# The same steps in a new order: replacing the written-out schedule of a two-branch kernel (attention with memory, and a long convolution)

## The chip, the cores and the metric

The kernel runs on 1 core of one Trainium2 chip. The metric is device time in microseconds (us), the median of several executions. Lower is better. A core has PE (TensorE, the matrix unit, with PEld its weight loads), ACT (ScalarE), DVE (VectorE), POOL (GpSimd) and SP (SyncE, which here issues every transfer). Each takes its own instructions strictly in order and waits for the others through semaphores.

## What is computed

The input `A_x` has 2048 tokens of 512 channels. The output is a gated mix of two branches. Cut to what matters:

```python
g = sigmoid((x * gate_w).sum(-1, keepdims=True))
a = A(x)      # 32 heads of 16; four segments of 512 tokens
b = B(x)      # a long convolution over the 2048 tokens, per channel
return g * a + (1 - g) * b

# A, for segment s and each head:
p = softmax(q @ k.T * scale + causal_mask)
o = gh * (phi(q) @ M) / (phi(q) @ z) + (1 - gh) * (p @ v)
M, z = M + phi(k).T @ v, z + phi(k).sum(0)     # memory for the next segment
a = o @ wo
# B:
K[d, l] = real(sum over n of C[d,n] * exp(dt[d] * A[d,n] * l) * dt[d] * B[d,n])
b = causal_conv(x, K) + x * Dskip              # by Fourier transforms in the reference
```

## The kernel before, in words

**Attention.** `do_xT` (L710) brings x transposed into memory: segment 0 by a plain load and PE transposes (L728), segments 1 to 3 by one transposing transfer each, issued on SP at L713. `project` (L979) makes q and k for one of four head groups of 8 heads, `seg_tokens` (L918) makes v. `scores` (L1008) runs five tiles per head group and segment, 80 in all. Each is a set of score matmuls into four PSUM banks (the same four every time), one exponential on ACT over 128 x 2048 (L1069), a causal mask (added by PE before the exponential in the first eight head groups, multiplied in by DVE at L1081 in the last eight), and the products with v. `norm` inside it ends with the DVE multiplication at L1044. `seg_state` (L937) updates the memory and `ophase` (L1100) adds the memory's part and transposes the outcome for the last product.

**Convolution.** `ssm_prep` (L734) and `ssm_powers` (L785) compute complex exponentials and then square them repeatedly, ten times in two halves; every power gets a table tile, of which a part is copied by a transfer inside the on-chip memory (the "copies of the power tables"). `tables` (L1136) multiplies them out on DVE (L1164, L1167, L1171) and PE turns them into kernel values ("lag"). `x_level1` (L845) makes the first transform level of x and stores it to a scratch in memory. `tail` (L1221) then goes through 16 frequency groups for each of two halves of the channels ("a" and "b"). For each group SP loads three operands (two parts of a constant named c_DNM, and the scratch), PE makes X and K, both are evicted, the halves of X are swapped by two 64 KB transfers, DVE multiplies (L1273), PE makes the inverse step V, and that is evicted and moved to its rows by a transfer.

**End.** Sixteen output blocks, eight per half, each add the attention's last product (`fina`, `finb`: all heads and segments must be there) and the convolution's last transform (`fira`, `firb`) in one PSUM bank. The two evictions of a block multiply by the gate (L229 on ACT, L230 on DVE) and every second block stores 256 KB.

**What sets the order.** All matmuls are recorded through one helper line (L687), and all plain transfers through L222. `evac` (L224) records a PSUM eviction that can run either on ACT (L226, or L229 with a scale) or on DVE (L227, or L230). The graph holds 1798 steps, numbered in the order in which the program records them. A string `ORDER` (L366 to L456) lists all 1798 numbers: `build_kernel` (L1362) reads it and `replay` (L235) goes through it. The text after a number gives slots, that is which buffer of a pool or which PSUM bank a new tile gets, and the letter a or v puts an eviction on ACT or DVE:

```python
order.append((int(w[0].rstrip("av")), "ACT" if w[0][-1] == "a" else "DVE", [int(v) for v in w[1:]]))
...
for T in o.tiles:
    if T.slot is None:
        T.pool.take(T, next(slots))
```

So each engine's queue is the list cut down to that engine's steps. A step waits for the steps whose outcome it reads, and for the former users of the slots it takes; `emit` (L264) writes the semaphores. SP waits as well: a transfer that is not ready holds all that stand behind it on SP.

## Time and profile before

| what | value |
|---|---|
| runs (median; lowest to highest) | 313.3 us; 310.99 to 313.7 |
| profiled execution: span | 311.0 us |
| lowest run beside it | 310.99 us |
| PE, DVE, ACT busy | 264.8, 260.2, 262.7 us |
| first score exponential begins, last one ends | 24.5, 274.5 us |
| transfers issued on SP | 283 |

How to read it: the slices of the page divide the span in 40 parts and give each engine's busy share in tenths. The windows give busy time and instruction counts of each engine in chosen stretches, the granted PE clock, and the DMA engines' share and rate. A group is one source line on one engine with its count, busy time, mean duration in ns, and the idle time just before its instructions with what ended it. Of a transfer, the timeline's row on SP is the time that SP was held by the issue, not the time until the data landed. The last exponential's end is the end of the row of L1069 that begins at 272.66 and takes 1.88 us.

### The profile page before, as it was taken

To read this page: it belongs to the slowest core of one execution; us is meant where nothing else is said; L and a number is where in the kernel's file an instruction comes from. 1 tells how busy PE (TensorE), PEld (TensorE's weight loads), DVE (VectorE), ACT (ScalarE), POOL (GpSimd) and SP (SyncE) were. 2 spreads that over 40 slices of the span, in tenths; PEclk is the share of its full clock that TensorE was granted. 3 is DMA by queue.
4 is the path that set the end of the run, shared out by engine and by line. 5 is a ranking of instruction groups with operands and counts; after the bars stand their busy time and mean duration, and the time that the engine had idled before them with its cause. 6 is when DMAs were issued, how large, how long until landed. Compare 5 with 4: busy or idle time off the path is not lost.

```text
span 311.0 us, 10366 instructions
## 1 busy us (share of the span) xinstructions
PE 264.8 (85%) x4397; PEld 185.1 (60%) x4430; DVE 260.2 (84%) x642; ACT 262.7 (84%) x320; POOL 3.1 (1%) x9
## 2 busy tenths in 40 slices
PE   2678788788779789998999898999999988799991
PEld 1433355454435547676766574676677666579991
DVE  1999899999998889998999868888999898862152
ACT  2999999999999979987999898999999999861150
POOL 2000000000000000000001000000000000000000
PEclk9995689999968779999999999999999999979997
DMA  6878522431232545465555657637555667511143
GB/s 145 280 176 160 142 87 70 124 118 52 83 110 77 160 121 155 147 197 157 158 173 192 199 159 229 196 95 228 156 197 186 200 200 217 168 52 48 38 137 102
DMA packets 54926, 45.82 MB, mean 147 GB/s; under 512 B 22624, under 2 KB 50272, under 8 KB 54880
## 3 DMA queue, kind: packets, MB, share of 16 engines
q1 hardware_dynamic: 54880, 45.16, 49.8%
q8 instruction: 35, 0.57, 0.8%
q14 instruction: 11, 0.09, 0.1%
HBM read 26.92 MB, written 6.29 MB: 107 GB/s over the span
## 4 chain that ended last, share of the span: by engine, by line
ACT 42%; PE 41%; issue 7%; DVE 4%; DMA 3%; SPq 1%; another core or an unknown queue 0%; DVEq 0%; ACTq 0%
PE psum L687 40%; ACT sb L1069 23%; ACT sb L226 13%; ACT sb L795 2%; DMA sb<-sb 1%; DVE sb L227 1%; DMA sb<-c_DNM 1%; DMA sb<-c_ident 1%; SPq L222 1%; ACT sb L803 1%; ACT sb L1000 1%; DVE sb L1273 1%; ACT sb L949 1%; DVE sb L1121 0%; ACT L888 0%
## 5 line engine op out<-in xcount | busy, mean ns | idle before, releaser
L687 PE MATMUL psum<-sb 128*128 128x17 bf16 (+12 forms) x4309 | 257.5, 225 | 32.5 <-ACT sb L1069 14.4
L687 PEld LDWEIGHTS psum<-sb 128*128 128x128 bf16 (+3 forms) x4342 | 178.2, 97 | 109.7 <-issue 29.7
L1069 ACT ACTIVATE sb<-psum 128x2048 bf16<-128x2048 f32 x80 | 151.9, 1899 | 6.7 <-PE psum L687 6.4
L226 ACT ACTIVATE sb<-psum 128x512 bf16<-128x512 f32 (+2 forms) x155 | 88.1, 625 | 8.6 <-PE psum L687 8.1
L227 DVE CAST sb<-psum 128x512 bf16<-128x512 f32 (+1 forms) x47 | 31.3, 676 | 4.8 <-PE psum L687 4.8
L1164 DVE TENSOR_TENSOR sb<-sb 128x512 bf16<-128x512 bf16 (+3 forms) x52 | 33.5, 654 | 0.0
L1167 DVE TENSOR_TENSOR sb<-sb 128x512 bf16<-128x512 bf16 (+3 forms) x52 | 33.3, 650 | 0.0
L1171 DVE TENSOR_TENSOR sb<-sb 128x512 bf16<-128x512 bf16 (+3 forms) x52 | 33.3, 656 | 0.0
L1081 DVE TENSOR_TENSOR sb<-sb 128x1024 bf16<-128x1024 bf16 (+1 forms) x40 | 22.5, 575 | 3.4 <-ACT sb L1069 3.3
L1273 DVE TENSOR_TENSOR sb<-sb 128x1024 bf16<-128x1024 bf16 x32 | 21.6, 678 | 2.6 <-DMA sb<-sb 1.9
L230 DVE TENSOR_SCALAR sb<-psum,sb 128x256 bf16<-128x256 f32 x18 | 8.4, 482 | 16.4 <-PE psum L687 15.2
L229 ACT ACTIVATE sb<-psum,sb 128x256 bf16<-128x256 f32 x14 | 6.2, 472 | 16.8 <-PE psum L687 8.8
L1044 DVE TENSOR_TENSOR sb<-psum,sb 128x256 bf16<-128x256 f32 x32 | 13.3, 418 | 0.3
L795 ACT ACTIVATE sb<-sb 128x512 f32<-128x512 f32 x18 | 11.6, 658 | 0.0
L1041 DVE RECIPROCAL sb<-psum 128x16 f32<-128x16 f32 x32 | 8.0, 251 | 2.3 <-PE psum L687 2.0
L1121 DVE TENSOR_TENSOR sb<-psum,sb 128x512 bf16<-128x512 f32 x12 | 8.2, 686 | 0.2
L743 PE MATMUL psum<-sb 128*128 128x128 bf16 x24 | 3.0, 310 | 6.0 <-DMA sb<-c_ident 5.4
L796 DVE TENSOR_TENSOR sb<-sb 128x256 f32<-128x256 f32 x18 | 7.5, 418 | 0.6 <-ACT sb L795 0.5
L949 ACT ACTIVATE sb<-psum 128x512 bf16<-128x512 bf16 x12 | 7.5, 622 | 0.3 <-PE psum L946 0.3
L1000 ACT ACTIVATE sb<-sb 128x512 bf16<-128x512 bf16 x12 | 7.5, 629 | 0.0
L227 DVE COPY sb<-psum 128x1024 bf16<-128x1024 bf16 x3 | 2.1, 686 | 6.4 <-PE psum L743 6.4
L797 DVE SCALAR_TENSOR_TENSOR sb<-sb 128x256 f32<-128x256 f32 x18 | 7.4, 415 | 0.0
(66 smaller groups left out, 102.0 us busy)
## 6 DMA issues: line engine op xcount, KB each, us to landing
sb<-c_DNM SPq DMA_DIRECT2D x32, 320.0 KB, 3.5
sb<-c_DNM SPq DMA_DIRECT2D x32, 192.0 KB, 3.0
sb<-sb SPq DMA_DIRECT2D x84, 64.0 KB, 2.6
scr_Z<-sb SPq DMA_DIRECT2D x16, 256.0 KB, 2.3
sb<-scr_Z SPq DMA_DIRECT2D x32, 128.0 KB, 3.1
sb<-sb SPq DMA_DIRECT2D x32, 128.0 KB
sb<-in_A_x_dram SPq DMA_DIRECT2D x5, 512.0 KB, 4.6
out_dram<-sb SPq DMA_DIRECT2D x8, 256.0 KB, 2.2
```

Of the source, the lines that this page charges most:

```text
L226: fa = lambda e: e.activation(dst(), src(), ACT.Copy)
L227: fd = lambda e: e.tensor_copy(dst(), src())
L687: mm = lambda e, o_, l, r_, st, sp, **kw: e.matmul(o_, lhsT=l, rhs=r_, start=st, stop=sp, skip_group_check=True, **kw)
L795: op("ACT", ("As", 512), lambda e, sq=sq, Z=Z: e.activation(ap(sq, n=512), ap(Z, n=512), ACT.Square), r=[Z], w=[sq], key=PW[h] + PWS * k)
L949: op("ACT", ("Ax", 512), lambda e: e.activation(ap(ek, n=512), ap(P, n=512), ACT.Exp), r=[P], w=[ek])
L1044: op("DVE", ("V1", 256), lambda e: e.tensor_tensor(ap(o1, gi * 16, [[128, 4], [32, 4], [1, 16]]), ap(T, dims=[[68, 4], [17, 4], [1, 16]]), ...
L1069: o = op("ACT", ("Ax", 2048), lambda e, P=P, pT=pT: e.activation(ap(pT, n=2048), ap(P, n=2048), ACT.Exp, scale=0.25), r=[P], w=[pT])
L1081: op("DVE", ("V2", 128 * nb), lambda e, pT=pT, dims=dims: e.tensor_tensor(ap(pT, dims=dims + [[1, 128]]), ap(pT, dims=dims + [[1, 128]]), ...
L1164: op("DVE", ("V2" if n > 1 else "V1", 256 * n), lambda e: e.tensor_tensor(run(tile, ne, dst, 1), run(tile, ne, src, sstep), ap(pw, cl * 51 ...
L1167: op("DVE", ("V2" if n > 1 else "V1", 256 * n), lambda e: e.tensor_tensor(run(t2, n, 0, 1), run(tile, ne, src, sstep), ap(pw, cl * 512 + 2 ...
L1171: op("DVE", ("V2" if n > 1 else "V1", 256 * n), lambda e: e.tensor_tensor(D_(), D_(), ap(t2, n * 128, [[-n * 128, 2], [2 * n, 64], [1, 2 * ...
L1273: op("DVE", ("V2", 1024), lambda e, Y=Y, XAB=XAB, K3=K3: e.tensor_tensor(ap(Y, dims=[[512, 2], [1, 512]]), ap(XAB, dims=[[512, 2], [1, 512 ...
```

## The change

Only the string `ORDER` is replaced. The same 1798 numbers stand in another order, with other slots, and other letters for the evictions. The change's own words: "Same steps, memory and transfers; order of all steps, engines of evictions and slots written anew, with the time that SP takes to begin each transfer counted in". Nothing of a step itself changes.

```diff
 ORDER = """
-9/0 10/1 391/1 15/0 29/0 0/0 23/0/0 24v 30/1 193/0 13/4 14/2 21/0 12/3 11/5 27/1/1 25/2/2 189/0 54/0 31/8 32/0 33/6
-38/2 39/3 57/3 34 190 35 7/0 37/11 20/0 1226/1 28a 36 17/0 45/8 40/4 41 55/4 44/5 26v 46/7 42 173/7 43 48/0 50/9 18/0
...
+9/0 10/1 0/0 23/0/0 24v 15/0 29/0 31/0 32/1 38/2 39/3 37/4 30/5 40/6 33/7 41 14/2 13/3 34 42 35 27/1/1 43 12/4 28a
+11/5 36 21/0 189/0 190 54/0 25/2/2 26a 173/0 7/0 49/8 53/0 176/0 45/9 50/10 44/11 48/1 46/12 47 51/13 52 57/3 177/0
...
```

What the two strings make of the queues, counted from them:

| what | before | after |
|---|---|---|
| instructions of PE steps, ACT, DVE, SP | 551, 317, 642, 283 | 551, 303, 656, 283 |
| output evictions on ACT (L229) / DVE (L230) | 14 / 18 | 0 / 32 |
| evictions of X, K and V of the tail on ACT, of 96 | 61 | 59 |
| q and k evictions on ACT | 30 of 32 | 26 of 32 |
| ACT instructions ahead of the first score exponential | 30 | 36 |
| ACT instructions up to and with the last one | 298 | 298 |
| identity load, place on SP | 4th | 3rd |
| loads of wq, wk, wv, places on SP | 18th, 14th, 15th | 13th, 14th, 16th |
| the three transposes, places on SP | 19th, 26th, 32nd | 15th, 20th, 28th |
| segment that each of them brings | 1, 2, 3 | 1, 3, 2 |
| first copy of a power table on SP | 22nd | 21st |
| first step of `tables` on DVE (a copy into a table) | 60th | 65th |

## The prediction

> **What bounds the kernel now.** I read the page first: busy shares, slices, costliest groups.

> ```profile
> span 311.0 us, 10366 instructions
> PE 264.8 (85%) x4397; PEld 185.1 (60%) x4430; DVE 260.2 (84%) x642; ACT 262.7 (84%) x320; POOL 3.1 (1%) x9
> DVE  1999899999998889998999868888999898862152
> ACT  2999999999999979987999898999999999861150
> L687 PE MATMUL psum<-sb 128*128 128x17 bf16 (+12 forms) x4309 | 257.5, 225 | 32.5 <-ACT sb L1069 14.4
> L1069 ACT ACTIVATE sb<-psum 128x2048 bf16<-128x2048 f32 x80 | 151.9, 1899 | 6.7 <-PE psum L687 6.4
> L226 ACT ACTIVATE sb<-psum 128x512 bf16<-128x512 f32 (+2 forms) x155 | 88.1, 625 | 8.6 <-PE psum L687 8.1
> L227 DVE CAST sb<-psum 128x512 bf16<-128x512 f32 (+1 forms) x47 | 31.3, 676 | 4.8 <-PE psum L687 4.8
> L1273 DVE TENSOR_TENSOR sb<-sb 128x1024 bf16<-128x1024 bf16 x32 | 21.6, 678 | 2.6 <-DMA sb<-sb 1.9
> L230 DVE TENSOR_SCALAR sb<-psum,sb 128x256 bf16<-128x256 f32 x18 | 8.4, 482 | 16.4 <-PE psum L687 15.2
> L229 ACT ACTIVATE sb<-psum,sb 128x256 bf16<-128x256 f32 x14 | 6.2, 472 | 16.8 <-PE psum L687 8.8
> ```

> Three engines have the same 260 us of work in 311 us, and ACT and DVE are full nearly everywhere but at both ends. ACT's row is a chain of 80 score exponentials (L1069, 1.90 us each) with evictions between them, so I use these "exps" as milestones, and read busy time in windows that begin where the 1st, 25th, 29th, 33rd, 37th, 45th, 53rd and 80th begin.

> ```profile
> core 0: us, PE busy (x) PEld busy (x) DVE busy (x) ACT busy (x) POOL busy (x), PEclk, DMA share, GB/s
> 0.00:24.50 24.50, 13.66 (x109) 8.32 (x112) 17.66 (x55) 18.20 (x33) 1.88 (x7) 0.98 0.74 203
> 24.50:102.30 77.80, 63.83 (x1243) 36.60 (x1256) 74.55 (x192) 75.89 (x96) 0.00 (x0) 0.87 0.38 100
> 102.30:116.30 14.00, 10.74 (x174) 6.76 (x160) 11.56 (x38) 11.90 (x15) 0.00 (x0) 0.76 0.49 140
> 116.30:133.00 16.70, 16.32 (x233) 12.07 (x234) 16.21 (x31) 15.78 (x23) 0.00 (x0) 1.00 0.51 150
> 133.00:152.60 19.60, 17.96 (x476) 14.00 (x475) 18.56 (x56) 16.49 (x24) 0.00 (x0) 1.00 0.60 186
> 152.60:178.50 25.90, 23.54 (x471) 16.30 (x473) 24.86 (x45) 24.22 (x30) 1.22 (x2) 1.00 0.58 176
> 178.50:204.60 26.10, 23.84 (x393) 16.75 (x396) 20.67 (x52) 24.33 (x28) 0.00 (x0) 1.00 0.64 189
> 204.60:272.70 68.10, 63.24 (x981) 45.95 (x985) 62.03 (x150) 65.22 (x59) 0.00 (x0) 1.00 0.61 185
> 279.00:304.60 25.60, 25.45 (x260) 23.33 (x260) 8.80 (x19) 7.04 (x16) 0.00 (x0) 1.00 0.26 78
> ```

> Window length less ACT busy is ACT's idle time: 6.3 us before the first exp, 1.9 up to the 25th, then 2.1, 0.9, 3.1, 1.7 and 1.8 in the five windows to 204.6, and 2.9 to the last exp. So ACT sets the time of the last exp (272.7), with 14.4 us of idle on the way, 9.6 of it from 102.3 to 204.6, where the convolution's steps come in. From 279 PE alone works: the 16 output blocks, which need all attention heads. SP's transfers hardly show. The rows of DMA issues (size, median us from issue to landing), and of waits for them (us in total, times, longest), are:

> ```profile
> sb<-sb SPq DMA_DIRECT2D x84, 64.0 KB, 2.6
> sb<-c_DNM SPq DMA_DIRECT2D x32, 192.0 KB, 3.0
> DVE sb L1273 <- DMA sb<-sb: 1.9, 4, 1.3
> PEld psum L687 <- DMA sb<-c_DNM: 0.7, 1, 0.7
> ```

> **The change, part by part.** All 1798 steps stay; their order on every engine, the eviction engine and the slots change. I counted each engine's new queue, pricing every instruction at its own duration in the profiled execution (an overlap with its predecessor taken off), or, where it changed engine, at the mean of its shape there.

> *ACT's work.* 303 evictions and activations instead of 317; the 14 output evictions at L229 (6.2 us in all) go to DVE. Those lay behind the last exp, under PE's last 25 us, so they buy nothing. Up to and with the last exp both queues hold 298, 250.0 us before and 250.6 after (mainly 6 fewer evictions of 512, and 2 more of 1024, 2 more copies of 512 and 4 of 256): +0.6 us on the path.

> *DVE's work.* 642 to 656 instructions, 260.2 to 267.4 us; up to the last normalisation (L1044 of the last head group) 249.3 to 251.4. In the last part DVE takes all 32 output evictions: 32 x 0.48 = 15.4 us beside PE's 25.5, hidden. What would lay this open is an output block waiting for its PSUM bank; with two evictions (0.96 us) to 1.6 us of PE per block that does not occur.

> *The start.* These rows of the timeline (start, length, what) carry it.

> ```profile
> 2.33 0.43 SPq L222 DMA_DIRECT2D sb<-c_ident  x1
> 5.37 1.92 PE L743 MATMUL psum<-sb 128*128 128x128 bf16 x16 [5.37 <-DMA sb<-c_ident]
> 6.44 0.69 DVE L227 COPY sb<-psum 128x1024 bf16<-128x1024 bf16 x1 [6.44 <-PE psum L743]
> 6.96 0.23 ACT L865 ACTIVATE sb<-sb 128x32 f32<-128x32 bf16 x1 [1.16 <-DMA sb<-in_A_beta_dram]
> 7.96 0.95 ACT L763 ACTIVATE sb<-sb 128x256 f32<-128x256 f32 x2 [0.77 <-DVE sb L762]
> 8.82 1.01 ACT L226 ACTIVATE sb<-psum 128x1024 bf16<-128x1024 bf16 x1
> 10.15 1.28 ACT L772 ACT_TABLE_LOAD   x1
> 11.85 5.99 SPq L713 DMA_TRANSPOSE sb<-in_A_x_dram  x1
> 23.59 3.56 SPq L713 DMA_TRANSPOSE sb<-in_A_x_dram  x1
> 30.10 3.08 SPq L713 DMA_TRANSPOSE sb<-in_A_x_dram  x1
> ```

> The identity moves from fourth to third on SP, one issue or 0.54 us earlier, and the first PE, DVE and L763 steps with it (L763 to about 7.1, since L865 now stands behind it). ACT then does two evictions of 1024 (1.0 each) instead of one ahead of its table load, which falls at about 9.6 instead of 10.15. Idle on ACT up to the load: 10.15 - 2.9 of work - 1.28 for the first load = 6.0 before; 9.6 - 3.5 - 1.28 = 4.8 after. I take 0.9 us of these 1.2. ACT then has 36 instructions (18.5 us) instead of 30 (14.5) ahead of the first exp, so that starts at 24.5 + 4.0 - 0.9 = 27.6. That is work done earlier, no loss.

> *SP.* 283 transfers in both. The three transposes stood 19th, 26th and 32nd in SP's queue and stand 15th, 20th and 28th; they hold SP for 5.99, 3.56 and 3.08 us, while nothing behind them goes out. Moved past: the loads of wv, of the block mask and of the mask column by the first, three copies of the power tables and two stores to the scratch by the second. Followed by hand (about 0.54 us per plain issue, the first transpose held for 6 us as the first row shows behind full loads, the second for 3.6 to 6), the first two hold SP from 8.3 to about 14.5 and from 17.5 to 21 or 23, wv lands near 19 (wanted at 21), and the first copy near 24 to 27 (wanted by DVE at 29, behind 21.1 us of its work). The third cannot go out before a copy that waits for DVE's 60th instruction (28.6): issue 29.9, landing 36 by the third row. Its first reader, the gates of segment 2, stands 30th in PE's queue and waits for an eviction on ACT until 37.7 anyway. Queued behind it on PE are the projection and the scores that ACT's 53rd and 55th instruction need. Cover is 1.7 us; beyond it each us of delay is one on ACT. I take nothing for it; the ends are 0 and, if the third holds as long as the first (5.99 for 3.3), 2.7 - 1.7 = 1 us of loss.

> [...]

> *The middle.* For the same exps, work of ACT / DVE / PE in us, old to new (DVE and PE: what must be done before the exp can run; PE at 0.43 ns per column, near the 0.44 of the window 279 to 304.6, 25.45 us for 58,368 columns, and short ones at 27 ns):
> - exps 1 to 29: ACT 87.8 to 86.8, DVE 83.0 to 83.7, PE 62.1 to 63.4
> - 29 to 33: ACT 15.8 to 15.2, DVE 16.2 to 14.0, PE 15.8 to 14.9
> - 33 to 37: ACT 16.6 to 19.0, DVE 22.9 to 22.0, PE 16.6 to 19.5
> - 37 to 45: ACT 24.2 to 23.2, DVE 24.1 to 23.3, PE 22.6 to 21.5
> - 45 to 53: ACT 24.3 to 21.7, DVE 21.0 to 22.1, PE 22.7 to 21.7
> - 53 to 80: ACT 65.2 to 64.6, DVE 62.0 to 63.8, PE 59.4 to 60.2

> In the old order DVE's work ahead of the 37th to 45th exp exceeds ACT's by 3 us, and there ACT waits; in the new one DVE stays 0.5 us below at the first exp and 1.2 or more afterwards. In return 33 to 37 carries more of ACT and PE at once.

> *The sum*, each stretch its fullest engine plus the idle of that engine in the old window: first exp 27.6; to the 29th 86.8 + 4.0 = 90.8; 15.2 + 0.9 = 16.1; PE 19.5 + 1.6 = 21.1; DVE 23.3 + 1.0 = 24.3; 21.7 + 1.8 = 23.5; 64.6 + 2.9 = 67.5. The last exp starts at 270.9 instead of 272.7. From there 38.3 us were left; PE's work behind the last exp falls from 29.5 to 28.8 us, of which I count the 0.4 that stood among the output blocks (one inverse step, 1024 columns): 37.9. Span 308.8, or 2.2 less. The span, 311.0, is that of the fastest of the three runs; the median, 313.3, lies 2.3 above. So 313.3 - 2.2 = 311.1.

> **The rivals.**
> *The middle flows.* If DVE's lead is all that stopped ACT, idle from 102.3 to 204.6 falls to the share of the two long windows (1.9 + 2.9 of 145.9 us, 3.3%): 3.4 us instead of the 8.0 in my sum, 306.5. For it: from 24.5 to 102.3 ACT runs at 98% beside a DVE at 96%. Against it: PE is at 92 to 98% from 116 to 152, and the wait rows of L1069 and L226 name PE, not DVE.
> *Transfers come late.* Place: the operand loads of the convolution (c_DNM) and the half swaps (sb<-sb 64 KB) ahead of L1273. For each transfer I added the work of the waiting engine between the last instruction that the transfer must wait for and the one that uses it: under 4 us in 14 cases before, 22 after. Each us missing is a stall. If a transfer takes 4 us with its issue, what is missing sums to 10.8 us before and 15.7 after, 4.9 more; at 4.5 us 20.6 and 28.2, 7.6 more: 318.7. It makes the kernel slower by over 1% from about 4.1 us on. Against it: the rows say 2.6 and 3.0 us, and only 2.6 us of waits; for it: those are medians, and the new order gives SP's queue in tighter sequence.
> *Nothing moves.* ACT's work is the same to 0.6 us, SP's cost was hidden, and the gains at the start go in new waits: 313.3. [...]

> **How the numbers follow.** My forecast has 0.46, the free middle 0.24, late transfers 0.22, nothing 0.08. About 1% is what a measurement of this kernel can tell from no change: 310.2 to 316.4. The forecast's own range is 308 to 314, some 0.16 of its chance below 310.2. Faster: 0.24 + 0.16 = 0.40; within: 0.30 + 0.08 = 0.38; slower: 0.22. The range goes from 303 (the free middle, with the rest of the start's gain and some more) to 317.5, which leaves the worst late transfers out.

> **What would show it.** First exp at 27 to 28.5; ACT idle from the 29th to the 53rd exp under 7 us (7.5 before); the 33rd to 37th exp the one stretch that lengthens (20 to 22 us); the last exp at 270 to 272; PE's last block of work again 25 us, with all evictions at L230. Wrong: a wait on a DMA among the longest waits of PE or DVE; the gates of segment 2 later than 39; ACT idle above 16 us between the first and the last exp.

## The result, and the profile after

The changed kernel takes 329.6 us (median of 4 runs, 327.33 to 331.56); the kernel before, run beside it, 312.85 (310.99 to 313.7). The ratio is 1.0523 [1.0449, 1.0596]: 5.2% slower, 16.8 us, where 311.1 was forecast. A ratio leaves out executions over 1.5% above the fastest of their kernel, a median does not, so the two can differ. The profiled execution has a span of 329.6, 18.6 more than the one of before.

The page of the changed kernel, first the engines and the slices, then groups, then the queue that brings instructions:

```profile
span 329.6 us, 10405 instructions
PE 274.6 (83%) x4430; PEld 186.2 (56%) x4430; DVE 269.4 (82%) x656; ACT 258.1 (78%) x306; POOL 3.2 (1%) x9
ACT  3999979978999289896999949899998998680000
PEclk9999789979996759999999979999999999699998
L687 PE MATMUL psum<-sb 128*128 128x17 bf16 (+11 forms) x4342 | 268.1, 230 | 40.2 <-ACT sb L1069 15.0
L1069 ACT ACTIVATE sb<-psum 128x2048 bf16<-128x2048 f32 x80 | 151.2, 1890 | 11.3 <-PE psum L687 10.5
L226 ACT ACTIVATE sb<-psum 128x512 bf16<-128x512 f32 (+2 forms) x149 | 85.2, 622 | 12.1 <-PE psum L687 11.6
L227 DVE CAST sb<-psum 128x512 bf16<-128x512 f32 (+1 forms) x55 | 36.5, 673 | 9.7 <-PE psum L687 8.7
L230 DVE TENSOR_SCALAR sb<-psum,sb 128x256 bf16<-128x256 f32 x32 | 14.4, 480 | 9.7 <-PE psum L687 9.2
q8 instruction: 35, 0.57, 0.8%
```

The work is close to what the prediction counted: ACT 258.1 busy, DVE 269.4 (267.4 counted), all 32 output evictions on DVE. What grew is idle time. ACT's slices have a 2 and a 4 where before they were 7 or more, and PEclk, the granted clock, dips close to them. The windows, cut at the 1st, 25th, 29th, 33rd, 37th, 45th, 53rd and 80th exponential as in the prediction, show where:

```profile
core 0: us, PE busy (x) PEld busy (x) DVE busy (x) ACT busy (x) POOL busy (x), PEclk, DMA share, GB/s
0.00:28.60 28.60, 15.74 (x73) 7.53 (x74) 20.45 (x61) 22.29 (x39) 1.87 (x7) 1.00 0.78 200
28.60:116.90 88.30, 68.62 (x1314) 38.98 (x1313) 73.45 (x194) 75.56 (x96) 0.66 (x1) 0.87 0.34 87
116.90:129.40 12.50, 10.98 (x159) 7.41 (x157) 10.96 (x31) 11.71 (x13) 0.00 (x0) 0.68 0.41 116
129.40:145.70 16.30, 16.24 (x225) 12.21 (x222) 16.02 (x34) 15.27 (x21) 0.00 (x0) 1.00 0.48 145
145.70:168.40 22.70, 19.51 (x480) 14.18 (x479) 19.27 (x51) 18.83 (x30) 0.00 (x0) 1.00 0.59 173
168.40:197.00 28.60, 24.09 (x543) 16.52 (x542) 23.35 (x45) 23.57 (x28) 0.65 (x1) 0.94 0.50 152
197.00:221.10 24.10, 22.68 (x323) 15.42 (x321) 21.78 (x57) 22.00 (x23) 0.00 (x0) 1.00 0.68 197
221.10:292.40 71.30, 66.70 (x984) 47.20 (x983) 63.29 (x144) 64.73 (x56) 0.00 (x0) 0.95 0.59 177
298.50:324.10 25.60, 24.53 (x253) 22.50 (x251) 15.72 (x36) 0.00 (x0) 0.00 (x0) 1.00 0.29 87
```

ACT's work up to the last exponential is 254.0 us, 252.0 before. Its idle time from the first to the last one is 32.1 us (12.7, 0.8, 1.0, 3.9, 5.0, 2.1, 6.6), 14.4 before. So 17.7 us of idle and 2.0 of work put the last exponential at 292.4 instead of 272.7. The rest of the kernel is 1.1 us shorter (37.2 from there to the end, 38.3 before).

Whom did ACT and DVE wait for? The rows of the waits (us in total, times, longest), first before, then after:

```profile
ACT sb L226 <- PE psum L687: 9.8, 15, 1.7
DVE sb L227 <- PE psum L687: 6.8, 10, 1.9
PE psum L687 <- issue: 6.5, 13, 1.3
ACT sb L1069 <- PE psum L687: 6.4, 14, 1.5
```

```profile
ACT sb L226 <- PE psum L687: 21.1, 14, 6.3
DVE sb L227 <- PE psum L687: 19.3, 13, 7.5
PE psum L687 <- issue: 13.1, 5, 3.0
ACT sb L1069 <- PE psum L687: 10.5, 22, 2.3
```

On ACT's and DVE's evictions there are about as many waits as before (14 for 15, 13 for 10), but single ones of 6.3 and 7.5 us, and PE itself stood five times for 13.1 us with "issue" as releaser: nothing that the profile shows held it. They belong together. `tables` ends, for each of four groups of 128 channels, in eight PE steps ("lag" steps) of 32 weight loads and 32 matmuls of 20 columns each, 512 instructions in all. The old order puts other steps between them (five, `oT`, one, two score steps, two for the second group); the new one has all eight in a row, except in the last group. In the timeline of the changed kernel (start, length, what, and in brackets the idle time before and its releaser) the second group looks like this, PE first, then ACT, then DVE:

```profile
106.33 2.02 PE L687 MATMUL psum<-sb 32*128 32x384 bf16 x136 [0.36 <-ACT sb L1069]
111.19 1.35 PE L687 MATMUL psum<-sb 128*32 128x20 bf16 x128 [2.83 <-issue]
115.19 1.72 PE L687 MATMUL psum<-sb 128*32 128x20 bf16 x16 [2.65 <-issue]
107.31 1.88 ACT L1069 ACTIVATE sb<-psum 128x2048 bf16<-128x2048 f32 x1
115.45 0.79 ACT L226 ACTIVATE sb<-sb 128x256 bf16<-128x256 bf16 x2 [6.26 <-PE psum L687]
116.95 1.88 ACT L1069 ACTIVATE sb<-psum 128x2048 bf16<-128x2048 f32 x1 [0.42 <-PE psum L687]
107.48 0.43 DVE L1044 TENSOR_TENSOR sb<-psum,sb 128x256 bf16<-128x256 f32 x1
115.45 0.57 DVE L227 COPY sb<-sb 128x256 bf16<-128x256 bf16 x3 [7.54 <-PE psum L687]
```

The group begins at 107.2 and ends at 115.4, with two halts. ACT has one exponential in hand (1.88 us); next in its queue stand copies into the table that the lag steps read, so they must wait for the last lag step. DVE has the same next. At the fourth group the wait is of another kind: no table is left to copy into, but the eviction for which ACT waits 3.31 us up to 192.3 belongs to an inverse step (Va11) that stands behind six lag steps in PE's queue. The kernel before, at the same group:

```profile
103.62 0.42 PE L687 MATMUL psum<-sb 128*32 128x20 bf16 x37 [1.20 <-issue]
104.30 1.53 PE L687 MATMUL psum<-sb 32*128 32x512 bf16 x40 [0.26 <-ACT sb L1069]
102.33 1.92 ACT L1069 ACTIVATE sb<-psum 128x2048 bf16<-128x2048 f32 x1
104.13 0.47 ACT L226 ACTIVATE sb<-sb 128x256 bf16<-128x256 bf16 x1
```

Its halt of 1.20 us lies under an exponential, and ACT never stops. The groups by line and form give the sum over all four groups, first before, then after; behind the first bar stand busy time and mean, behind the second the idle time ahead:

```profile
L687 PE MATMUL psum<-sb 128*32 128x20 bf16 x1024 | 10.5, 176 | 2.8 <-issue 2.5 <-DVE sb L1171 0.2
```

```profile
L687 PE MATMUL psum<-sb 128*32 128x20 bf16 x1024 | 10.1, 178 | 13.1 <-issue 13.1
```

The lag steps hold PE for 13.3 us in the old order and 23.2 in the new one, at the same work. One more place stands out, at 272 to 278:

```profile
272.20 0.43 SPq L222 DMA_DIRECT2D sb<-in_A_wo_dram  x1
277.77 0.69 DVE L1273 TENSOR_TENSOR sb<-sb 128x1024 bf16<-128x1024 bf16 x1 [1.66 <-DMA sb<-sb]
278.19 1.32 PE L687 MATMUL psum<-sb 128*128 128x256 bf16 x26 [1.64 <-DMA sb<-c_DNM]
```

The load of wo (512 KB) stood 267th on SP and now stands 251st, ahead of the half swaps and the c_DNM operand of groups that are due. From the 75th to the 77th exponential 8.7 us pass, 4.8 before.

### The profile page after: what moved, and what is told of

Same layout as the page of the kernel before. It is cut to its first block, busy times and chain, and to the rows that moved or that the text cites. A ratio compares the mean times of both kernels' runs of the same rounds, so it can differ in the third digit from the quotient of the medians.

```text
span 329.6 us, 10405 instructions
## 1 busy us (share of the span) xinstructions
PE 274.6 (83%) x4430; PEld 186.2 (56%) x4430; DVE 269.4 (82%) x656; ACT 258.1 (78%) x306; POOL 3.2 (1%) x9
## 4 chain that ended last, share of the span: by engine, by line
PE 50%; ACT 30%; issue 8%; DVE 4%; DMA 3%; SPq 2%
PE psum L687 49%; ACT sb L1069 16%; ACT sb L226 9%; ACT sb L795 2%; SPq L222 2%; DVE sb L227 2%; DMA sb<-sb 1%; DMA sb<-in_B_B_re_dram 1%; DMA sb<-c_DNM 1%; ACT sb L949 1%; DVE sb L1081 1%; ACT sb L803 1%; DVE sb L1273 0%; ACT L949 0%; ACT L772 0%
## 5 line engine op out<-in xcount | busy, mean ns | idle before, releaser
L687 PE MATMUL psum<-sb 128*128 128x17 bf16 (+11 forms) x4342 | 268.1, 230 | 40.2 <-ACT sb L1069 15.0
L687 PEld LDWEIGHTS psum<-sb 128*128 128x128 bf16 (+3 forms) x4342 | 179.2, 98 | 125.5 <-issue 39.0
L1069 ACT ACTIVATE sb<-psum 128x2048 bf16<-128x2048 f32 x80 | 151.2, 1890 | 11.3 <-PE psum L687 10.5
L226 ACT ACTIVATE sb<-psum 128x512 bf16<-128x512 f32 (+2 forms) x149 | 85.2, 622 | 12.1 <-PE psum L687 11.6
L227 DVE CAST sb<-psum 128x512 bf16<-128x512 f32 (+1 forms) x55 | 36.5, 673 | 9.7 <-PE psum L687 8.7
L1171 DVE TENSOR_TENSOR sb<-sb 128x512 bf16<-128x512 bf16 (+3 forms) x52 | 33.9, 663 | 0.1
L1167 DVE TENSOR_TENSOR sb<-sb 128x512 bf16<-128x512 bf16 (+3 forms) x52 | 33.7, 658 | 0.0
L1164 DVE TENSOR_TENSOR sb<-sb 128x512 bf16<-128x512 bf16 (+3 forms) x52 | 33.6, 660 | 0.0
L1273 DVE TENSOR_TENSOR sb<-sb 128x1024 bf16<-128x1024 bf16 x32 | 21.8, 681 | 3.4 <-DMA sb<-sb 2.6
L230 DVE TENSOR_SCALAR sb<-psum,sb 128x256 bf16<-128x256 f32 x32 | 14.4, 480 | 9.7 <-PE psum L687 9.2
L1044 DVE TENSOR_TENSOR sb<-psum,sb 128x256 bf16<-128x256 f32 x32 | 13.3, 418 | 0.4
L227 DVE COPY sb<-sb 128x256 bf16<-128x256 bf16 x12 | 2.6, 292 | 10.6 <-PE psum L687 10.6
L226 ACT ACTIVATE sb<-sb 128x256 bf16<-128x256 bf16 x8 | 3.1, 445 | 9.5 <-PE psum L687 9.5
L743 PE MATMUL psum<-sb 128*128 128x128 bf16 x24 | 3.1, 311 | 5.7 <-DMA sb<-c_ident 4.0
## 6 DMA issues: line engine op xcount, KB each, us to landing
sb<-c_DNM SPq DMA_DIRECT2D x32, 192.0 KB, 2.9
```

The costliest lines, as they stand in the source:

```text
L226: fa = lambda e: e.activation(dst(), src(), ACT.Copy)
L227: fd = lambda e: e.tensor_copy(dst(), src())
L230: fd = lambda e: e.tensor_scalar(dst(), src(), scale(), None, ALU.mult)
L687: mm = lambda e, o_, l, r_, st, sp, **kw: e.matmul(o_, lhsT=l, rhs=r_, start=st, stop=sp, skip_group_check=True, **kw)
L1044: op("DVE", ("V1", 256), lambda e: e.tensor_tensor(ap(o1, gi * 16, [[128, 4], [32, 4], [1, 16]]), ap(T, dims=[[68, 4], [17, 4], [1, 16]]), ...
L1069: o = op("ACT", ("Ax", 2048), lambda e, P=P, pT=pT: e.activation(ap(pT, n=2048), ap(P, n=2048), ACT.Exp, scale=0.25), r=[P], w=[pT])
```

## The experiments

Three theories run through the expectations, under the names that they had when each was written. **Supply** (later S): the dense lag runs are halted for want of instructions, and these halts are what the change costs. **Place** (A in the later ones): the loss sits at the lag groups, because what needs their results stands right behind them on ACT and DVE. The rival to both (B): the loss is spread over the whole order, and the lag groups cost both kernels about the same. Beside them stands **T**, the early load of wo. The kernel before, run beside the experiments, took 311.66 to 313.43 us; each ratio is to that. The 13.5 and 6.2 us of gaps in the first expectations are read on PE's weight loads, those of other steps included; the rows above, of the lag matmuls alone, say 13.1 and 2.5.

### Half of the lag work, in both kernels

The second matmul of each pair is left out in both, so the convolution's kernel values come from half of their sum.

```diff
-for cc in range(2):
+for cc in range(1):
...
-                                       ap(F, ..., [[2, NF]]), cc == 0, cc == 1, tile_position=(0, 32 * dq))
+                                       ap(F, ..., [[2, NF]]), True, True, tile_position=(0, 32 * dq))
```

> The new order; the second matmul of every lag pair is left out, so that the kernel values lack one of their two terms, and a run of 8 steps has 256 instructions instead of 512. Supply: the gaps without a releaser at the lag runs fall below 1 us each, 317 to 322 us. Rival, PE's time in the run: only half the steps' own busy time goes (32 steps of 0.28 us, halved: 4.5 us at most), the gaps stay, 325 to 329.

> The kernel before with the second matmul of each pair of the lag steps left out (the same edit that took the changed kernel from 329.6 to 315.0 us): a control. Theory A (the changed order loses its time at the lag groups, because the steps that need their results stand right behind them on ACT, DVE and PE): before has cover there, so it gains far less than 14.6 us: 303 to 309 us. Rival B (lag work costs both orders the same, the difference lies elsewhere): it gains 12 to 16 us too, 296 to 300.

Changed kernel: 314.98 us, ratio 1.0042 [0.9996, 1.0088], 14.7 us less. Kernel before: 309.12, ratio 0.9922 [0.9898, 0.9946], 2.5 less. So some 12 of the 16.8 us hang on the lag groups (12.1 by the medians, 12.6 by the ratios), and B is out for these. The edit took more than expected off the changed kernel, the kernel before came out just above the 303 to 309 of A, and not every halt fell below 1 us: one of 3.1 stayed in the second group.

```profile
L687 PE MATMUL psum<-sb 128*32 128x20 bf16 x512 | 5.2, 178 | 3.1 <-issue 3.1
```

The edit halves columns and instructions at once, which the next pair separates.

### Half of the instructions, all of the columns

The same matmuls are left out, but those left stream their 20 columns twice; the second 20 go where the next matmul writes. Again half of the sum is missing.

```diff
-i = mm(e, ap(P, sl * NF, n=NF, p0=32 * dq, np_=32), ...
-       ap(F, cc * FPL + (dl // 2) * 2 * NF + dl % 2, [[2, NF]]), ...
+i = mm(e, ap(P, sl * NF, n=2 * NF, p0=32 * dq, np_=32), ...
+       ap(F, cc * FPL + (dl // 2) * 2 * NF + dl % 2, [[0, 2], [2, NF]]), ...
```

> The changed kernel with half the instructions of the lag steps and all of their columns: the second matmul of each pair is left out, and the first one streams its 20 columns twice (40 columns, the second 20 written into the place that the next matmul overwrites). TensorE streams as many columns as before in these runs, from 256 instead of 512 instructions. Theory S (the supply of instructions makes the lag runs long: 13.1 us of issue idle ahead of 10.1 us of matmuls): 315 to 319 us, near the 315.0 of the kernel with half the matmuls and half the columns, and the issue idle of these matmuls falls to 3 to 5 us. Rival W (the matmul work of the runs, uncovered on ACT and DVE, costs most): 322 to 328.

> The same edit in the kernel before: half the instructions of the lag steps, all of their columns. There the issue idle ahead of the lag matmuls is 2.8 us. Theory S: 309 to 312 us, at most the 2.5 us that halving instructions and columns gave. Rival W: 311 to 314, no gain at all.

Changed kernel: 316.31 us, ratio 1.0110 [1.0051, 1.0169]. Kernel before: 310.13, ratio 0.9903 [0.9866, 0.9940]. The lag matmuls and the instruction queue of the changed kernel with this edit:

```profile
L687 PE MATMUL psum<-sb 128*32 128x40 bf16 x512 | 5.3, 186 | 3.4 <-issue 3.4
q8 instruction: 31, 0.51, 0.7%
```

And of the kernel before with it:

```profile
L687 PE MATMUL psum<-sb 128*32 128x40 bf16 x512 | 5.8, 185 | 0.2
```

The columns cost next to nothing: 512 matmuls of 40 columns keep PE busy for 5.3 us, as 512 of 20 did in the pair above (5.2), and the intervals of the two pairs overlap. It is the number of instructions that counts, in two ways: 4.8 us of busy time and 9.7 us of issue idle went, 14.5 together, and the kernel gained 13.3. In the kernel before 4.7 and 2.6 went, 7.3 together, and it gained 3.3: there more than half was covered. Rival W is out as it was meant, with the columns as the work. But PE's busy time went down as well, since it follows the instructions, so up to 4.8 of the 13.3 us can be work of the lag steps and not halts; this edit does not part the two.

The q8 rows say what the supply is. 35 transfers of 16 KB for 4430 weight loads and 4430 matmuls are 253 of these per block; with 3918 of each it is 31 blocks, 253 again. So this queue feeds PE, some 253 instructions to a block. A block's packets took 0.9 to 2.2 us in the traces of the two kernels. In a lag group that does not halt, 256 instructions went in 1.2 us.

The traces also show that the halts are waits for these blocks. In the changed kernel the packets of a block end at 73.26, 109.72, 113.64, 151.28 and 190.10 us, and PE goes on at 74.66, 111.19, 115.19, 152.66 and 191.35. In all traces of this case 40 lag matmuls have an issue idle of over 0.3 us, and each of them starts 0.9 to 1.6 us after the end of a block (the eight in the traces of the two kernels 1.2 to 1.6), though blocks come some 9 us apart on average.

### Joining, splitting and spreading the lag steps

PE's queue is what changes; with it, steps on ACT and DVE move by up to 3 and 8 places in the split and by up to 15 on DVE in the single version. First the kernel before with the second and third group joined (its ACT, DVE and SP queues stay; the fourth group changes too, from 3+1+2+2 to 4+4 lag steps, though the expectation says that it stays); then the changed kernel with the old grouping; then the kernel before with two other steps between any two lag steps. PE's queue at the second group:

```diff
 (before: joined)
-sc1.0.B1 lag1 lag1 lag1 lag1 lag1 oT0.2 lag1 sc1.0.C sc1.0.C lag1 lag1 sc1.1.A1
+sc1.0.B1 lag1 lag1 lag1 lag1 lag1 lag1 lag1 lag1 oT0.2 sc1.0.C sc1.0.C sc1.1.A1
 (after: split)
-sc1.0.B1 lag1 lag1 lag1 lag1 lag1 lag1 lag1 lag1 sc1.0.C sc1.0.C st1.1 pv1.0.B0
+sc1.0.B1 lag1 lag1 lag1 lag1 lag1 sc1.0.C lag1 sc1.0.C st1.1 lag1 lag1 pv1.0.B0
 (before: single)
+sc1.0.B1 lag1 oT0.2 sc1.0.C lag1 sc1.0.C sc1.1.A1 lag1 sc1.1.A1 pv1.0.C lag1 ...
```

> The old order, with the lag steps of the second and third channel group in one run of 8 each (the first and the last stay 4+4 because of their PSUM banks). Supply: two or three gaps of 2.4 to 3 us appear there, 317 to 321 us. Late transfers, or the order as a whole: 312 to 314.

> The new order, with the 32 lag steps of PE (each 32 weight loads and 32 matmuls) broken up as in the old order (4+4, 5+1+2, 3+5, 3+1+2+2 instead of 8, 8, 8, 6+1+1). Theory, instruction supply: PE's instructions arrive in blocks of 16 KB and a run of 512 of them in some 3 us outruns this; the five gaps of 13.5 us in all that have no releaser shrink to the old order's 6.2, and what waits behind them on ACT and DVE with them: 319 to 322 us. Rival, late transfers: these runs do not matter, 328 to 331. Rival, the order as a whole: 327 to 331.

> The old order, with two other PE steps between any two lag steps. Supply: the old order's own gaps (6.2 us in five) fall to 1 to 3 us, 307 to 311. Late transfers, or the order as a whole: 312 to 315, the tables of the next channel group being a little later.

Joined, before: 322.13 us, ratio 1.0302 [1.0228, 1.0377], a little above the range of the supply theory. Only the places of lag steps on PE changed, and the loss is 9.4 us by the ratio. Its lag matmuls:

```profile
L687 PE MATMUL psum<-sb 128*32 128x20 bf16 x1024 | 10.4, 178 | 8.2 <-issue 8.2
```

Issue idle grew by 5.7 us (2.5 to 8.2), and the time by more. Of the halts, 1.4 and 3.1 us fall in the second and third group and 3.2 in the regrouped fourth, so the loss is not that of the two joined groups alone. Nor did the groups get longer: the last three run for 4.4, 5.4 and 9.1 us, against 5.2, 5.9 and 9.7. ACT's two longest waits, 5.6 us up to 144.2 and 5.3 up to 188.1, are for an inverse step and a score step that stand behind lag steps in PE's queue. Bringing the lag steps closer together is enough to make the old order slow.

Split, after: 329.73 us, ratio 1.0580 [1.0506, 1.0654]: no gain, and the supply theory in its simple form (fewer halts, less time) misses.

```profile
L687 PE MATMUL psum<-sb 128*32 128x20 bf16 x1024 | 10.4, 177 | 6.1 <-issue 6.1
```

The halts shrank from 13.1 to 6.1 us. But the second group now runs from 108.2 to 116.3 instead of 107.2 to 115.4: the steps put between have taken the time that the halts gave back, and DVE's copies still wait for the end, for 7.59 us (7.54 in the changed kernel).

Single, before: 336.46 us, ratio 1.0770 [1.0698, 1.0843], where 307 to 311 was expected. The run with the profile is the longest of four (340.34 us; mean granted clock 0.875, where the other three have 0.905 to 0.924 and those of the kernel before 0.939 to 0.963). In it the issue idle of the lag matmuls is down to 0.6 us, but the four groups last 11.9, 12.5, 18.0 and 12.2 us (4.8, 5.2, 5.9 and 9.7 in the kernel before), ACT waits 31.7 us at L226, and the granted clock of PE falls:

```profile
PEclk9996599955878559996589999799999999979998
```

So it isn't the halts alone that cost, nor the number of steps in a row. As the waits read, what costs is how late PE comes to what stands next on ACT and DVE: to the last lag step, whose result they need, or to a step that stands behind the lag steps in PE's queue. Halts are one way to make it late, other steps between are another. The old grouping sits between the two. No run varies this lateness alone, so this reading is argued from the waits.

### The load of wo

Its issue goes twelve places later on SP; in the second kernel half of the lag matmuls are left out as well.

```diff
-SP: ... Vb8 Zxb12 ld_wo Xb14 Xb10 CTb15 Vb7 ... Xb14 Zxb13 Vb10
+SP: ... Vb8 Zxb12 Xb14 Xb10 CTb15 Vb7 ... Xb14 Zxb13 ld_wo Vb10
```

> The changed kernel with one issue moved: the load of wo (512 KB) goes out twelve places later on SP, behind the swaps of Xb10, Xb14, CTb15 and Zxb13, as it stands in the kernel before. Theory T (late transfers at 273 to 278 us hold DVE 1.66 us and PE 1.63 us, and the drop of the PE clock that follows costs the rest): 325.5 to 327.5 us, and ACT's idle time between the 75th and the 80th exponential falls from 4.7 us to under 2. Rival (ACT and DVE wait there for something else at once): 328.5 to 330.5.

> The changed kernel with both single edits that gained: the second matmul of each lag pair left out, and the load of wo issued twelve places later on SP. If the two losses are separate (Theory A: 14.7 us at the lag groups, 3.2 us at wo's load) they add up: 311 to 313 us, 2 to 4 above the kernel before with the same matmuls left out (309.1). Rival (the late transfers only hurt because the lag groups made everything late): 314 to 316.

326.41 us, ratio 1.0494 [1.0445, 1.0542], and 312.55, ratio 1.0017 [0.9974, 1.0059], both within the ranges of T and A. By medians 3.2 and 2.4 us, by ratios 0.9 and 0.8; the intervals overlap those without the edit, so the size is open between these. That the place is mended is plain. From the 75th to the 77th and to the 80th exponential, with wo later:

```profile
275.50:280.30 4.80, 4.42 (x75) 3.17 (x76) 4.59 (x13) 4.74 (x5) 0.00 (x0) 1.00 0.67 200
280.30:288.20 7.90, 6.44 (x114) 4.73 (x115) 7.39 (x17) 6.17 (x6) 0.00 (x0) 1.00 0.66 184
```

ACT's idle time there is 0.06 and 1.7 us. In the changed kernel it was 4.7 (15.8 us from 276.6 to 292.4, 11.07 busy).

### New orders of the same steps

If the plan was wrong in what a lag group costs, a plan with better numbers should be faster. Six times I wrote the order of PE, ACT and DVE anew by durations from the traces, with engines, slots and SP's order kept: once in four stretches only, three times for the kernel before, twice for the changed one. The second plan for the kernel before counts three things besides the durations: when a step of ACT or DVE starts that needs the result of the step right ahead of it, half clock behind windows in which PE does little, and the blocks of instructions. The last plan of each kernel also prices a PE step by the kind of step ahead of it. The edit is always in `ORDER` alone; for the second group it reads, in the first plan and in the last one for the kernel before:

```diff
 (changed kernel, four stretches)
+sc1.0.B1 lag1 lag1 lag1 st1.1 lag1 sc1.0.C sc1.0.C lag1 oT0.3 lag1 pv1.0.C lag1 lag1 sc1.1.A1
 (kernel before, last plan)
+sc1.0.B1 lag1 lag1 lag1 pv1.0.B0 lag1 sc1.0.C oT0.2 sc1.0.C lag1 lag1 lag1 lag1 st1.1 pv1.0.C sc1.1.A1
```

> The changed kernel with the order of PE, ACT and DVE steps written anew only inside four stretches around the lag groups (62 to 84, 98 to 124, 141 to 164 and 180 to 200 us), by the durations of its own trace, with each dense lag run given the 2 to 3 us that the instruction blocks make it wait; SP's order, engines, slots and everything outside the stretches stay. PE's runs become 3+1+4, 3+1+1+1+2, 2+2+4 and 3+1+3+1 with scores between, no PE step moves by over 13 places. Theory A (the loss sits at the lag groups): 317 to 322 us, and ACT's idle time at the 53rd exponential falls from 35.7 to under 28. Rival B (the loss is spread over the whole order): 326 to 330.

> The kernel before with its engines, slots and SP's order kept, and the order of PE, ACT and DVE steps written anew by the durations of its own trace and the waits of its lag runs for instruction blocks. Theory A (a plan that prices the lag groups as the chip ran them holds on the chip): 302 to 307 us, faster than both kernels. Rival (the trace's durations hold for its own order alone, as the clock and the supply of instructions move with the order): 310 to 316.

> [...] Theory A (these three and the measured durations make the difference between an order that reads well and one that runs well): 300 to 307 us. Rival (an order fitted to one trace does not hold in another): 312 to 330.

> The changed kernel, with its engines of evictions, its slots and SP's order kept, and only the order of PE, ACT and DVE steps written anew in the same way as e9, by the durations of its own trace. Theory A (the loss lies in the order of steps around the lag groups, not in engines, slots or SP's order): 302 to 310 us, at least 19 us below the changed kernel. Rival (engines, slots or SP's order hold a good part of the loss): 315 to 326.

> The kernel before, engines, slots and SP's order kept, PE, ACT and DVE steps in a new order once more. [...] Theory A (the price of PE's steps was what the plans had wrong, as it was in the changed kernel's middle): 300 to 309 us, faster than both kernels. Rival (no order fitted to one trace holds in another, whatever is counted): 315 to 332.

> The changed kernel, engines, slots and SP's order kept (wo's load still early), PE, ACT and DVE steps in a new order by the same prices as e12. Theory A (the loss lies in the order of PE, ACT and DVE alone): 310 to 319 us. Rival (engines, slots or SP's order of the changed kernel hold it at its time): 325 to 335, as e10 gave.

Measured: 334.08, 334.48, 331.07, 333.50, 326.39 and 333.50 us, ratios 1.0647 [1.0556, 1.0739], 1.0727 [1.0688, 1.0765], 1.0557 [1.0458, 1.0656], 1.0637 [1.0533, 1.0741], 1.0426 [1.0352, 1.0499] and 1.0676 [1.0584, 1.0768]. Every expectation of a gain failed; four of the six came out above the rival's range as well. In these traces the issue idle of the lag matmuls is between 0.2 and 5.0 us, where the kernel before has 2.5, so the halts of the lag steps alone cannot be what holds them. The last plan for the kernel before loses most of it early: its first exponential comes at 30.6 us and its ninth at 60.7 (24.5 and 51.8), and its clock is low in these slices:

```profile
PEclk9969557999979977999799999999999999989997
```

What these runs show is that six of six plans from the durations of one trace did not hold on the chip. What they read from a trace moves with the order: up to the last exponential the changed kernel has 41.0 us at half clock and the kernel before 27.3, the halts of the lag matmuls are 13.1 and 2.5 us, and the first transpose holds SP for 7.24 and 5.99 us. The plans' own rules may be off: the last two count half clock after any window of 3.41 us with PE busy under 72%, which no run shows as a rule; in the traces of the kernel before and the changed one it followed 9 of 23 such windows between 25 and 298 us. What held each of the six was not separated, and no version faster than the kernel before was found.

## Why the prediction was wrong, point by point

The step that failed is **the sum**: "each stretch its fullest engine plus the idle of that engine in the old window". It treats the queues of a stretch as if they ran past each other, and lets the old idle time stand for all waits. What the runs show in its place is that the order inside PE's queue sets the waits: at the lag groups ACT and DVE stood idle until PE came to the step that they needed, and half of the lag work alone accounts for some 12 us of the loss. Forecast and measured length of each stretch:

| stretch | forecast | measured |
|---|---|---|
| to the first exponential | 27.6 | 28.6 |
| 1st to 29th | 90.8 | 100.8 |
| 29th to 33rd | 16.1 | 16.3 |
| 33rd to 37th | 21.1 | 22.7 |
| 37th to 45th | 24.3 | 28.6 |
| 45th to 53rd | 23.5 | 24.1 |
| 53rd to 80th | 67.5 | 71.3 |
| behind the 80th | 37.9 | 37.2 |

Of the 20.8 us between the spans 308.8 and 329.6, 10.0 fall in the stretch of the first two lag groups, 1.6 in that of the third and 4.3 in that of the fourth: 15.9. Halving the lag instructions took 13.3 us back (3.3 in the kernel before), most of the miss of 18.5. The 3.8 us of the stretch from the 53rd hold the load of wo.

The sum also leaves its own rule twice. From the 33rd to the 37th exponential its list has DVE as the fullest engine (22.0 us) and from the 45th to the 53rd too (22.1), but it adds PE and ACT there. With DVE and its old idle time, 1.0 and 5.4 us, these stretches would be 23.0 and 27.5: 5.9 us more in all, and still 14.9 short of the measured span. And the span is not that of the fastest run: in every run where both are on record it is 1.7 to 2.3 us below the time (329.6 for 331.4). The forecast uses the difference of spans alone, so this does not move it.

*ACT's work*: 2.0 us more to the last exponential, 0.6 forecast. Right in kind, and small.

*DVE's work*: right. From 298.5 to 324.1 PE is busy for 24.53 of 25.6 us, with all 32 output evictions (14.4 us) beside it.

*The start*: 28.6 for 27.6. The gain of 0.9 us on ACT's idle did not come: it is 6.3 us up to the first exponential, as before (28.6 less 22.29).

*SP*: right. The transposes hold it for 7.24, 3.51 and 2.01 us, the third goes out at 29.85 (29.9 forecast), and the gates of segment 2 run at 38.2. The step looked at the start alone, though. That wo's load moves from the 267th to the 251st place, past swaps and operands that were due, is in no step.

*The middle*: the price of the lag steps was not too low. 1024 matmuls at 27 ns are 27.6 us; they held PE for 23.2, and for 13.3 in the old order. (Matmuls of 17 columns start 25 to 26 ns apart in both traces, those of the lag steps some 9 ns apart where they do not halt.) So the sum priced the same steps alike in both orders, where the traces have them 9.9 us apart. What failed is the place. The eight lag steps were spread evenly over their stretch by the sum; in the queue they are a block of up to 8.2 us, in which PE feeds nobody, and what ACT and DVE have next needs its end. This could be read before: PE's new queue has eight lag steps in a row, the next two places on ACT are copies that wait for the last of them, and the old trace has the halts already in its group by form (2.5 us of issue).

*The signs named beforehand*: ACT's idle time between the first and the last exponential is 32.1 us, twice the 16 that were to show the forecast wrong; the 33rd to the 37th is not the one stretch that lengthens (19.6 to 22.7 us): the 1st to 29th goes from 91.8 to 100.8, the 37th to 45th from 25.9 to 28.6 and the 53rd to 80th from 68.1 to 71.3. ACT's idle time from the 29th to the 53rd is 12.0 us, where under 7 was to show the forecast right, and the last exponential comes at 292.4, not at 270 to 272.

*The rivals*: "Transfers come late" ends on the right side, but not by its mechanism. The c_DNM loads land in 2.9 us (3.0 before) and the swaps in 2.6 (2.6); only those behind wo's load made an engine wait for over 1 us. None of the three rivals had the lag groups in it.

**What stays open.** With half of the lag instructions in both kernels, 6.2 us are left between them (316.3 and 310.1), of which wo's load is 0.8 to 3.2. The rest was not assigned. How much of the loss at the lag groups goes through PE's clock was not measured by itself, as no edit here changes the clock alone. Up to the last exponential the changed kernel has 41.0 us at half clock, the kernel before 27.3. That this is not the whole of it shows in the kernel with four stretches written anew: it has 27.3 us too, a mean granted clock of 0.954, and a span of 327.4.

## What to carry to other kernels

Before adding up engines by stretch, go through the new queue for blocks: a run of steps on one engine that feeds nobody until its end, next to what the other engines have in hand until then. What the run takes longer than that work is idle time: 8.2 us less 1.9 gives the 6.3 that ACT waited at the second group. Count a run of very small matmuls by its instructions and not by its columns (512 of 40 columns kept PE busy for 5.3 us, 512 of 20 for 5.2, 1024 of 20 for 10.1), and look in the trace of before for idle time with the releaser "issue" on their row: the run of 512 instructions in the second group paid it twice, 2.83 and 2.65 us. A new order planned from the durations of one trace is a new experiment, not a forecast.
